# Storing the last three output tiles of an attention and feed-forward kernel from two queues in place of one

## The chip, the core and the metric

The kernel runs on one core of a Trainium2 chip. A core has four engines that compute: TensorE (PE, with its weight loads shown as PEld), VectorE (DVE), ScalarE (ACT) and GpSimd (POOL). SyncE (SP) computes nothing; in this kernel it issues nearly all transfers between the memory on the chip (SBUF) and the large memory outside it (HBM). [...] Each engine works through a list of its own in order. Engines wait for each other, and for transfers, by semaphores.

The metric is the device time of the core in microseconds (us), as the median of several executions. A profile is one further execution with the recorder on.

## What is computed

Attention over 576 positions with 16 extra "beacon" keys that every query may see, for 8 batches and 8 heads of width 64, followed by a gated feed-forward layer on the 4608 resulting rows:

```python
k_all = np.concatenate([beacon_k, k], axis=2)
v_all = np.concatenate([beacon_v, v], axis=2)
scores = scale * np.matmul(q, k_all.transpose(0, 1, 3, 2))
scores = np.where(causal, -1000000000.0, scores)
a = softmax(scores)
attn = np.matmul(a, v_all)                       # (8, 8, 576, 64)
x = attn.transpose(0, 2, 1, 3).reshape(4608, 512)
gate = np.maximum(x @ w_gate, 0.0)               # 512 -> 1536
val = x @ w_val
out = gate * val @ w_out                         # 4608 x 512, float32
```

## The kernel before

The attention's result is written, transposed, into one large tile `xT` (512 features in four groups of 128 partitions, 4608 columns). The feed-forward part takes the columns in pieces. For each batch it takes the first 512 of the 576 positions; the remaining 64 positions of the batches are gathered afterwards, four batches at a time, into two groups of 256 columns (the loop `for i in range(2)`, lines 899 to 908). The second of these groups (`i == 1`) is the last work of the kernel.

For a group of columns two functions are called:

- `hidden` (lines 822 to 843) computes the 1536 hidden features in 12 blocks of 128: four matmuls with `w_gate`, a Relu on ScalarE out of PSUM, four matmuls with `w_val`, and the product of both on VectorE, which goes to a tile `hT` in bfloat16.
- `project` (lines 845 to 867) multiplies the 12 `hT` tiles with `w_out` for 128 output rows: 12 matmuls into one PSUM bank (line 853), then one copy into an SBUF tile `osb` by ScalarE or VectorE (lines 861 and 862; the copy shows as line 438 on ScalarE and 440 on VectorE), then the stores to HBM (lines 864 to 867).

The 128 rows of a tile of the gathered groups belong to two batches, 64 rows each, which don't lie side by side in the output. Therefore such a tile has two stores of 64 rows (the list `rows` has two entries); a tile of the other kind has one store of 128 rows. The last tile of all is made in two halves of 256 columns (`LAST_PARTS = 2`), each with its own PSUM bank, copy and two stores. So the second gathered group ends with three output tiles: one of 128 x 512 and two of 128 x 256, and six stores.

Which engine does what, and in which order, is decided before the program is built. Each piece of work is a task with a set of engines that could do it, a cost, the tasks that it depends on, and a priority (class `Plan`, lines 146 to 264). The planner simulates the engines and repeatedly takes the task that could start earliest, the one of smallest priority value among equals. A copy may go to "ACT" or "DVE", whichever comes first in that simulation. Tasks of the engine "DMA" are issued by SP, with a simulated wire behind them. The order that the planner finds is the order of each engine's list. All six of the last stores are "DMA" tasks, so they stand in SP's list one after another.

An issue on SP ends when the transfer has been handed on; the transfer lands later and raises a semaphore. At the very end (the launch's line 941) SP waits for the landing of all transfers, one semaphore after another, and then the engines meet in a last barrier.

Of the kernel before, what the change touches and what calls it, by code (L numbers as in the profile page):

```python
# [51 lines left out]
OUT = -1300.0  # L52
# [93 lines left out]
class Plan:  # L146
# [7 lines left out]
    def add(self, engines, cost, run, deps=(), holds=(), prio=0.0, lag=None, part=False, lazy=0.0, after=0.0, move=0.0):  # L154
        t = Task(engines if isinstance(engines, tuple) else (engines,), cost, run, deps, holds, prio, lag, part, lazy, move)
        t.ready = after
        for d in t.deps:
            d.users.append(t)
        self.tasks.append(t)
        return t  # L160
# [107 lines left out]
def kernel(  # L268
# [12 lines left out]
    nc = tc.nc  # L281
    B, H, S, D = q.shape
# [4 lines left out]
    P = 128  # L287
# [65 lines left out]
    add = plan.add  # L353


    def c_dve(n):
        return 0.07 + 0.00104 * n
# [7 lines left out]
    def c_act(n):  # L365
        return 0.06 + 0.00083 * n
# [4 lines left out]
    def c_pe(n):  # L371
        return 0.003 + n / 2400.0
# [63 lines left out]
    def copy(e, dst, src):  # L436
        if e == "ACT":
            nc.scalar.copy(dst, src)  # L438
        elif e == "DVE":
            nc.vector.tensor_copy(dst, src)  # L440
        else:
            nc.gpsimd.tensor_scalar(dst, src, 1.0, 1.0, ALU.mult, ALU.mult)
# [379 lines left out]
    def hidden(rhs, w, c0, deps, hT, prio):  # L822
        hid = []
        for nf in range(NF):
            psg, psv, g = Hold(f_s, 2), Hold(f_s, 2), Hold(gate_s, 2)

            def product(w_r, ps, nf=nf):
                for ki in range(KM):
                    x = rhs(ki)
                    to = ps.tile[:, :w]  # L830
                    if len(x.shape) == 3:
                        to = to.rearrange("p (b s) -> p b s", b=x.shape[1])
                    nc.tensor.matmul(to, w_r[:, ki, nf * P:(nf + 1) * P], x, start=(ki == 0), stop=(ki == KM - 1))  # L833

            a = add("PE", 4 * c_pe(w), lambda _, f=product, ps=psg: f(wg_r, ps), deps + [weight_in["g", nf // 4]],
                    (psg,), prio + 0.02 * nf)
            r = add("ACT", c_act(w), lambda _, psg=psg, g=g: nc.scalar.activation(  # L837
                g.tile[:, :w], psg.tile[:, :w], AF.Relu), (a,), (psg, g), -1000 + prio)
            b_ = add("PE", 4 * c_pe(w), lambda _, f=product, ps=psv: f(wv_r, ps), [a, weight_in["v", nf // 4]],
                     (psv,), prio + 0.02 * nf + 0.01)  # L840
            hid.append(add("DVE", c_dve(w), lambda _, psv=psv, g=g, nf=nf: nc.vector.tensor_mul(  # L841
                hT[nf].tile[:, c0:c0 + w], g.tile[:, :w], psv.tile[:, :w]), (r, b_), (psv, g, hT[nf]), -1000 + prio))
        return hid

    def project(t0, rows, here, hT, prio, last):
        w = DM // LAST_PARTS if last else DM
        for n0 in range(0, DM, w):
            ps, osb = Hold(f_s, 4), Hold(osb_s, 1 + len(rows))
            prev = None
            for part in range(3):  # L850
                def outp(_, part=part, ps=ps, n0=n0):
                    for nf in range(4 * part, 4 * part + 4):
                        nc.tensor.matmul(ps.tile[:, :w], hT[nf].tile[:, t0:t0 + P], wo_r[:, nf, n0:n0 + w],  # L853
                                         start=(nf == 0), stop=(nf == NF - 1))

                need = [prev, weight_in["o", part]]
                for hid in here:
                    need += hid[4 * part:4 * part + 4] + (hid[:11] if part == 0 else [])
                prev = add("PE", 4 * c_pe(w), outp, need, (ps,) + tuple(hT[4 * part:4 * part + 4]),
                           prio + 0.3 + 0.01 * part + 0.001 * (n0 > 0) - (0.5 if part else 0))  # L860
            ev = add(("ACT", "DVE"), {"ACT": c_act(w), "DVE": c_dve(w)}, lambda x, ps=ps, osb=osb: copy(
                x.engine, osb.tile[:, :w], ps.tile[:, :w]), (prev,), (ps, osb), -1000 + prio)
            at = 0
            for r0, n in rows:
                add("DMA", (0.4, 0.78 * n / P), lambda _, osb=osb, r0=r0, n=n, at=at, n0=n0: nc.sync.dma_start(
                    out[r0:r0 + n, n0:n0 + w], osb.tile[at:at + n, :w]), (ev,), (osb,), prio + OUT)
                at += n


# [13 lines left out]
    def done(b, lo, hi):  # L883
        return [x for (b0, what, _), x in x_done.items() if b0 == b and SPAN[what][0] < hi and SPAN[what][1] > lo]

    REG = S // MT * MT
    for b in range(B):
        hT = [Hold(hid_s, len(CUTS.get(b, ())) + 1 + REG // P) for _ in range(NF)]
        cuts = [0, *CUTS.get(b, ()), REG]
        prio = 1000 + 10.0 * b  # L890
        here = []
        for a, z in zip(cuts, cuts[1:]):
            here.append(hidden(lambda ki, a=a, z=z, b=b: xT[:, ki, b * S + a:b * S + z], z - a, a, done(b, a, z), hT, prio))
            for t0 in range(a // P * P, z // P * P, P):
                project(t0, [(b * S + t0, P)], [x for x, c0, c1 in zip(here, cuts, cuts[1:]) if c0 < t0 + P and c1 > t0],
                        hT, prio, False)
            prio += 2.0
    ends = xT.rearrange("p k (b s) -> p k b s", s=S)
    for i in range(2):
        b0, b1 = i * B // 2, (i + 1) * B // 2  # L900
        w = (b1 - b0) * (S - REG)
        prio = 1000 + 10.0 * b1 - 5.0
        hT = [Hold(hid_s, 1 + w // P + (LAST_PARTS - 1) * i) for _ in range(NF)]
        deps = [x for b in range(b0, b1) for x in done(b, REG, S)]
        hid = hidden(lambda ki, b0=b0, b1=b1: ends[:, ki, b0:b1, REG:], w, 0, deps, hT, prio)
        for t0 in range(0, w, P):
            b = b0 + t0 // (S - REG)
            project(t0, [(x * S + REG, S - REG) for x in (b, b + 1)], [hid], hT, prio, i == 1 and t0 + P == w)

    def fill(n, to):  # L910
        for _ in range(n):
# [34 lines left out]
```

## Time and profile before

| | us |
|---|---|
| median of 3 runs | 409.17 |
| lowest and highest | 408.51, 409.42 |
| the profiled execution | 410.43 |
| its span, from the first to the last instruction | 408.7 |

The span is what the views of the profile divide up; all their times count from its start. The profiled execution took 1.73 us beyond its span. The page gives busy times by engine, a picture of the span in 40 slices of 10.2 us each, and the chain of work that ended last. A timeline row reads: start, duration, engine, line, operation, what it writes and reads, and in brackets how long the engine had been idle and who released it. SPq stands for SP's issues. The mean granted clock of TensorE was 0.997.

### The profile page before, as it was taken

The numbers are of one execution on the slowest core, as the hardware profiler recorded it, in microseconds if no ns is written. First come the engines' busy times: TensorE is split into PE (matmuls) and PEld (weight loads), VectorE is DVE, ScalarE is ACT, GpSimd is POOL, SyncE is SP. The second block draws the span as 40 slices with busy tenths as digits, with TensorE's granted clock in tenths as the row PEclk, the third lists the DMA queues.
The fourth block names the chain that finished last, engine by engine and source line by source line (L and its number), as shares of the span: only waits on it lengthen the run. The fifth ranks groups of instructions, "written<-read, shape, count | busy, mean of one in ns | idle before, by whom it ended". The sixth has DMA issues, their size and how long they took to land.

```text
span 408.7 us, 10376 instructions
## 1 busy us (share of the span) xinstructions
PE 394.1 (96%) x3276; PEld 246.8 (60%) x3311; DVE 315.8 (77%) x1159; ACT 289.9 (71%) x959; POOL 232.7 (57%) x434
## 2 busy tenths in 40 slices
PE   7899999989999999999999999999999999999994
PEld 5567867567766877555557754654554544444483
DVE  6898999889989988899998998787988544244251
ACT  6899989778888968797888799998867432033040
POOL 5899786947777667586975966875727200000000
PEclk9999999999999999999999999999999999999998
DMA  8899999999989999999999999999195730100112
GB/s 224 167 199 225 212 209 196 171 242 219 176 172 230 215 178 231 190 227 195 242 209 210 234 198 189 249 201 205 54 162 125 167 73 0 70 34 0 53 54 51
DMA packets 172616, 68.03 MB, mean 166 GB/s; under 512 B 146832, under 2 KB 168080, under 8 KB 172560
## 3 DMA queue, kind: packets, MB, share of 16 engines
q1 hardware_dynamic: 167808, 62.64, 75.5%
q0 software_dynamic: 4752, 4.72, 7.1%
q8 instruction: 26, 0.43, 0.5%
q14 instruction: 30, 0.25, 0.2%
HBM read 38.27 MB, written 9.44 MB: 117 GB/s over the span
## 4 chain that ended last, share of the span: by engine, by line
PE 84%; POOL 7%; DMA 2%; DVE 2%; ACT 2%; issue 2%; SPq 0%; POOLq 0%
PE f L833 42%; PE f L853 22%; PE f L663 7%; PE f L766 5%; PE f L497 4%; POOL xT L710 2%; POOL pb L710 2%; POOL h L486 2%; PE f L655 2%; DMA st<-in_beacon_k_dram 1%; PE f L795 1%; DMA st<-in_q_dram 1%; DVE diag L440 1%; PE f L745 1%; ACT xT L689 1%
## 5 line engine op out<-in xcount | busy, mean ns | idle before, releaser
L710 POOL TENSOR_SCALAR pb<-pb,small 128x576 bf16<-128x576 bf16 (+8 forms) x224 | 121.6, 557 | 56.0 <-DVE small L703 49.0
L689 ACT ACTIVATE pb<-f,small 128x64 bf16<-128x64 f32 (+6 forms) x256 | 131.0, 524 | 18.0 <-DVE small L678 13.1
L837 ACT ACTIVATE g<-f 128x512 f32<-128x512 f32 (+3 forms) x156 | 71.9, 470 | 67.9 <-PE f L833 66.6
L678 DVE CUSTOM_DVE_ANT_0 f<-f,mask 128x128 f32<-128x128 f32 (+7 forms) x256 | 112.0, 477 | 9.4 <-PE f L663 7.2
L833 PE MATMUL f<-xT,wv_r 128*128 128x512 bf16 (+3 forms) x616 | 111.8, 313 | 0.5
L833 PE MATMUL f<-xT,wg_r 128*128 128x512 bf16 (+3 forms) x619 | 109.5, 313 | 0.3
L841 DVE TENSOR_TENSOR hT<-g,f 128x512 bf16<-128x512 f32 (+3 forms) x156 | 80.5, 520 | 37.6 <-PE f L833 34.4
L853 PE MATMUL f<-wo_r,hT 128*128 128x512 bf16 (+1 forms) x423 | 102.0, 373 | 1.0
L833 PEld LDWEIGHTS <-wg_r 128*128 128x128 bf16 x624 | 60.0, 98 | 32.3 <-issue 0.2
L833 PEld LDWEIGHTS <-wv_r 128*128 128x128 bf16 x624 | 59.4, 98 | 33.0 <-issue 0.8
L853 PEld LDWEIGHTS <-hT 128*128 128x128 bf16 x444 | 41.6, 98 | 39.1
L689 ACT ACTIVATION_READ_ACCUMULATOR pb<-f,small 128x1 f32 x256 | 53.8, 210 | 0.0
L663 PE MATMUL f<-kT,diag 128*128 128x384 bf16 (+7 forms) x255 | 46.9, 286 | 1.9 <-DVE diag L440 0.8
L678 DVE DVE_READ_ACCUMULATOR2_ANT small<- 128x1 f32 x296 | 41.6, 141 | 0.2 <-issue 0.2
L486 POOL TENSOR_SCALAR h<-st 128x512 bf16<-128x512 f32 x62 | 37.8, 614 | 7.1 <-DMA st<-in_q_dram 2.9
L440 DVE COPY osb<-f 128x512 f32<-128x512 f32 (+1 forms) x26 | 17.6, 678 | 23.2 <-PE f L853 22.7
L710 POOL TENSOR_SCALAR xT<-xT,small 128x64 bf16<-128x64 bf16 (+4 forms) x64 | 26.9, 436 | 7.7 <-ACT xT L689 4.1
L497 PE MATMUL f<-ident,h 128*128 128x128 bf16 (+2 forms) x320 | 28.1, 217 | 2.8 <-POOL h L486 2.5
L438 ACT CAST diag<-f 64x512 bf16<-64x512 f32 (+2 forms) x52 | 23.0, 442 | 9.6 <-PE f L497 4.1
L497 PEld LDWEIGHTS <-h 128*128 128x128 bf16 (+2 forms) x320 | 20.3, 98 | 15.6 <-POOL h L486 7.9
L440 DVE CAST diag<-f 64x512 bf16<-64x512 f32 (+2 forms) x44 | 26.3, 598 | 4.2 <-ACT diag L438 2.0
L663 PEld LDWEIGHTS <-diag 128*128 128x128 bf16 x256 | 20.4, 98 | 15.0 <-issue 1.5
(67 smaller groups left out, 376.7 us busy)
## 6 DMA issues: line engine op xcount, KB each, us to landing
st<-in_q_dram SPq DMA_DIRECT2D x32, 256.0 KB, 4.5
st<-in_k_dram SPq DMA_DIRECT2D x32, 256.0 KB, 5.0
out_dram<-osb SPq DMA_DIRECT2D x32, 256.0 KB, 2.6
st<-in_v_dram SPq DMA_DIRECT2D x24, 256.0 KB, 4.7
st<-in_v_dram SPq DMA_DIRECT2D x8, 224.0 KB, 4.9
wg_r<-in_moe_w_gate_dram POOLq DMA_DIRECT2D x3, 512.0 KB, 8.5
wv_r<-in_moe_w_val_dram POOLq DMA_DIRECT2D x3, 512.0 KB, 10.3
wo_r<-in_moe_w_out_dram POOLq DMA_DIRECT2D x3, 512.0 KB, 14.2
```

Source lines behind the costliest of these rows:

```text
L438: nc.scalar.copy(dst, src)
L440: nc.vector.tensor_copy(dst, src)
L486: (nc.gpsimd if x.engine == "POOL" else nc.vector).tensor_scalar(to, of, by, 1.0, ALU.mult, ALU.mult)
L497: nc.tensor.matmul(to, h16.tile[:rows, a * P:(a + 1) * P], ident[:rows, :rows], start=True, stop=True)
L663: nc.tensor.matmul(view(i), t.diag.tile[:, p, j * P:j * P + P], kT[:, p, :n], start=True, stop=True)
L678: nc.vector.tensor_tensor_reduce(out=view(i), in0=view(i), in1=msk, scale=1.0, scalar=small["t"][:, 0:1] if name in "EF" else 3.0e38, op0= ...
L689: nc.scalar.activation(ph.tile.rearrange("p a n -> p (a n)")[:, a:a + n], view(i), AF.Exp, bias=small["t"][:, low:low + 1], scale=-1.0, ac ...
L710: (nc.gpsimd if x.engine == "POOL" else nc.vector).tensor_scalar(one, one, small["t"][:, 8 + i:9 + i], 1.0, ALU.mult, ALU.mult)
L833: nc.tensor.matmul(to, w_r[:, ki, nf * P:(nf + 1) * P], x, start=(ki == 0), stop=(ki == KM - 1))
L837: r = add("ACT", c_act(w), lambda _, psg=psg, g=g: nc.scalar.activation(g.tile[:, :w], psg.tile[:, :w], AF.Relu), (a,), (psg, g), -1000 + ...
L841: hid.append(add("DVE", c_dve(w), lambda _, psv=psv, g=g, nf=nf: nc.vector.tensor_mul(hT[nf].tile[:, c0:c0 + w], g.tile[:, :w], psv.tile[: ...
L853: nc.tensor.matmul(ps.tile[:, :w], hT[nf].tile[:, t0:t0 + P], wo_r[:, nf, n0:n0 + w], start=(nf == 0), stop=(nf == NF - 1))
```

## The change

`project` gets one more argument, `final`, which is true for the second gathered group alone. There, the store of the second 64 rows of a tile (`at` is 64 then) becomes a task of the engine "ACT" with a cost of 0.6, and the function that runs it issues the transfer on ScalarE's queue. All other stores stay as they were. The second gathered group has three tiles, so three stores move.

```diff
-    def project(t0, rows, here, hT, prio, last):
+    def project(t0, rows, here, hT, prio, last, final):
...
             for r0, n in rows:
-                add("DMA", (0.4, 0.78 * n / P), lambda _, osb=osb, r0=r0, n=n, at=at, n0=n0: nc.sync.dma_start(
-                    out[r0:r0 + n, n0:n0 + w], osb.tile[at:at + n, :w]), (ev,), (osb,), prio + OUT)
+                def store(x, osb=osb, r0=r0, n=n, at=at, n0=n0):
+                    (nc.scalar if x.engine == "ACT" else nc.sync).dma_start(out[r0:r0 + n, n0:n0 + w], osb.tile[at:at + n, :w])
+
+                if final and at:
+                    add("ACT", 0.6, store, (ev,), (osb,), prio + OUT)
+                else:
+                    add("DMA", (0.4, 0.78 * n / P), store, (ev,), (osb,), prio + OUT)
                 at += n
...
-                        hT, prio, False)
+                        hT, prio, False, False)
...
-            project(t0, [(x * S + REG, S - REG) for x in (b, b + 1)], [hid], hT, prio, i == 1 and t0 + P == w)
+            project(t0, [(x * S + REG, S - REG) for x in (b, b + 1)], [hid], hT, prio, i == 1 and t0 + P == w, i == 1)
```

## The prediction

> **What bounds the kernel now.** I read the page first: the span, the busy shares, the slices, the chain.
>
> ```profile
> span 408.7 us, 10376 instructions
> PE 394.1 (96%) x3276; PEld 246.8 (60%) x3311; DVE 315.8 (77%) x1159; ACT 289.9 (71%) x959; POOL 232.7 (57%) x434
> ...
> PE   7899999989999999999999999999999999999994
> ...
> DMA  8899999999989999999999999999195730100112
> ...
> PE 84%; POOL 7%; DMA 2%; DVE 2%; ACT 2%; issue 2%; SPq 0%; POOLq 0%
> ```
>
> TensorE is busy for 96% of the span and makes 84% of the chain. But its last slice of 10.2 us shows 4 tenths, and there the DMA engines wake up again. The change acts only in that slice, so I went on to the chain and the timeline of the end.
>
> ```profile
> 403.23 0.02 issue
> 403.26 0.42 DVE osb L440
> ```
>
> ```profile
> 401.51 0.69 DVE L440 COPY osb<-f 128x512 f32<-128x512 f32 x1 [2.97 <-PE f L853]
> 401.95 0.37 ACT L438 COPY osb<-f 128x256 f32<-128x256 f32 x1 [3.95 <-PE f L853]
> 403.26 0.42 DVE L440 COPY osb<-f 128x256 f32<-128x256 f32 x1 [1.05 <-PE f L853]
> ```
>
> The chain of waits ends at 403.68 (403.26 + 0.42), with the last copy out of PSUM, yet the span ends at 408.7. So 5.0 us lie behind the last computing instruction, where the chain follows nothing. There SyncE (SP) works off the stores. Its rows, one by one (start, duration of the issue):
>
> ```profile
> 402.23 0.51 SPq L865 DMA_DIRECT2D out_dram<-osb  x1
> 402.79 0.58 SPq L865 DMA_DIRECT2D out_dram<-osb  x1
> 403.46 0.55 SPq L865 DMA_DIRECT2D out_dram<-osb  x1
> 404.07 0.59 SPq L865 DMA_DIRECT2D out_dram<-osb  x1
> 404.75 0.55 SPq L865 DMA_DIRECT2D out_dram<-osb  x1
> 405.35 0.59 SPq L865 DMA_DIRECT2D out_dram<-osb  x1
> ```
>
> These are the stores of the last three tiles, two halves each; I call the tiles X (128x512), Y and Z (128x256) and the halves 1 (first 64 rows) and 2. X is ready at 402.20 (401.51 + 0.69) and Y at 402.32, but Y1 is issued at 403.46 only. Z is ready at 403.68 and Z1 goes out at 404.75, Z2 at 405.35: SP is behind by 1.1 and 1.7 us. The queue of issues, not the copies, sets the end. What follows the last issue:
>
> ```profile
> SPq L941 <- DMA out_dram<-osb: 1.4, 1, 1.4
> ```
>
> ```profile
> 403.38:404.78 1.40, 0.00 (x0) 0.00 (x0) 0.30 (x1) 0.00 (x0) 0.00 (x0) 1.00 0.92 200
> 405.30:405.78 0.48, 0.00 (x0) 0.00 (x0) 0.00 (x0) 0.00 (x0) 0.00 (x0) 1.00 0.64 137
> 405.94:406.42 0.48, 0.00 (x0) 0.00 (x0) 0.00 (x0) 0.00 (x0) 0.00 (x0) 0.84 0.64 137
> 406.58:407.05 0.47, 0.00 (x0) 0.00 (x0) 0.00 (x0) 0.00 (x0) 0.00 (x0) 0.50 0.65 140
> 383.50:384.40 0.90, 0.90 (x6) 0.42 (x5) 0.01 (x1) 0.00 (x0) 0.00 (x0) 1.00 0.81 298
> ```
>
> The last two numbers of a window are the DMA engines' share and GB/s. Z2's issue ends at 405.94, its 64 KB move from 406.58 to 407.05 (0.64 later, for 0.47), and SP, which waits from 405.98 or so, is released 1.4 later, at 407.40 (0.35 after the last packet). From there to the end of the span is 1.3 us of closing checks and barriers at line 941.
>
> **The change part by part.** In the order of the changed program, PE, VectorE and GpSimd have the same instructions in the same order; SP has three stores fewer; ScalarE gets X2, Y2 and Z2 behind its copy of Y, its last work. So nothing before 402 us moves, and nothing is queued behind the new stores on ScalarE but the closing barrier.
>
> *SP loses three issues.* X1 stays at 402.23 to 402.74. Y1 follows after the gap of 0.09 that stands between 403.37 and 403.46 (a second wait): 402.83, until 403.42 at the most. Then SP waits for Z's copy, and Z1 starts 0.03 after it, as X1 did after X's: 403.71. That is 1.64 us ahead of 405.35, where the last issue starts now.
>
> *ScalarE gains three issues.* No transfer of this program is issued on ScalarE, so the price is bounded by the nearest rows: 0.33 us (SP, a store of 128 rows) and 0.93 (GpSimd, loads of weights).
>
> ```profile
> L865 SPq DMA_DIRECT2D out_dram<-osb x4: 332/332/333, 382.7 to 388.7; - x4
> ```
>
> ```profile
> 16.09 0.93 POOL L455 DMA_DIRECT2D wg_r<-in_moe_w_gate_dram  x1
> ```
>
> I take SP's 0.51 to 0.59 for a store of 64 rows, the same shape on a like queue. X2 then starts between 402.23 and 402.35 (when the copy of Y ends), Y2 ends by 403.6, before Z is ready, and Z2 starts beside Z1 at 403.71. At 0.93 Z2 starts at 402.23 + 2 x (0.93 + 0.09) = 404.27 and lands at 404.27 + 0.93 + 0.64 + 0.47 + 0.35 = 406.66, still 0.74 before the present end.
>
> *The closing checks.* They take the landings one after another:
>
> ```profile
> L941 SPq EVENT_SEMAPHORE  x8: 28/28/28, 407.4 to 407.8; - x8
> ```
>
> Eight checks lie between 407.4 and 407.8. Z1 on SP keeps the place that is checked first, Z2 on ScalarE takes the last, so Z2 may land 0.4 later at no cost. The checks still run, 1.3 us in all.
>
> *The data.* Halves 1 and 2 of a tile now move at the same time. Z1 and Z2 end their issues at 404.22 to 404.30, and their packets start 0.64 later, at about 404.9. Whether they run side by side or one behind the other isn't in the trace, which has one queue. Below: side by side, 0.47, a landing at 404.86 + 0.47 + 0.35 = 405.68, a gain of 1.72. Above: all six stores packed behind one another at a full share of the engines, from 403.38: 1.40 x 0.92 + 4 x 0.48 x 0.64 = 2.52, to 405.90, a landing at 406.25, a gain of 1.15. A row speaks for the better half: a store of 128 rows (both halves) ran at 298 GB/s with a share of 0.81, the 64-row halves of X at 200 GB/s with 0.92, so halves of opposite partitions seem to get in each other's way less than rows of the same one. I take the middle, 1.45.
>
> [...]
>
> **Sum.** Against the profiled execution: 410.43 us, of which 408.7 is span and 1.73 lies around it; it becomes 408.98, its span 407.25. That execution is 1.26 above the median of 409.17, and I take the same difference there: 409.17 - 1.45 = 407.72.
>
> **The rivals.**
>
> *A, one descriptor generator for both queues.* The issues end at 402.74, 403.37, 404.01, 404.66, 405.30 and 405.94: 0.64 apart each time, though the gaps before them are 0.05 to 0.10. Longer gap, shorter issue (0.55 after 0.09, 0.59 after 0.06). Something behind SP keeps a pace of 0.64, and the first store, with nothing ahead of it, took only 0.51. If that something serves ScalarE too, with h per store, the sixth issue ends at 402.74 + 5h against 405.94: at h = 0.64 nothing is gained (409.17), at 0.585 0.27, at 0.51 0.65 (408.5). My value is 0.54, 0.50 gained, 408.7. Against it: loads of four times as much data show no such pace, three of them in 1.46, 0.49 each.
>
> ```profile
> 2.83 1.46 SPq L520 DMA_DIRECT2D st<-in_k_dram  x3
> ```
>
> So the 0.64 may as well be SP's own work on an odd shape. [...]
>
> *B, the data serialize.* If the DMA engines never overlap two of the six stores, they take 1.40 + 4 x 0.48 = 3.32 from 403.38, to 406.70, a landing at 407.05: 0.35 gained, 408.8. Against it: with a share of 0.64 in each burst there is room, and now already Y1's packets start while X2's end, since 1.40 reaches to 404.78 and Y1's issue ended at 404.01, 0.64 before 404.65.
>
> *C, slower: ScalarE's issues are long.* If one takes a, Z2 starts at 402.23 + 2(a + 0.09), and lands at 403.87 + 3a. It decides from 407.8 (with the 0.4 of the last check), at a = 1.31, and costs 3 us for each further us; from a = 1.58 the loss is over 0.2%. What speaks for it: this queue is used nowhere else in the program, and an issue of SP did take 2.47 once, early, behind a long row of loads:
>
> ```profile
> 9.51 2.47 SPq L562 DMA_DIRECT2D st<-in_k_dram  x1
> ```
>
> At 2.47 the loss is 3.48, 412.6. Against it: at the end no other transfer is under way, and all SP's stores take 0.33 to 0.59.
>
> **How the numbers follow.** My forecast 0.52; A 0.24; B 0.10; C 0.14. The predicted time is the forecast's, 407.7. Its own range is 1.15 to 1.72 gained, 407.45 to 408.0, and with the spread of the three runs (408.51 to 409.42, 0.45 to a side) 407.1 to 408.4. The range given goes on to A and B, whose slowest is 409.17, and the spread: 407.1 to 409.6; C is left out. 0.2% is 0.82 us, about what a measurement of this kernel can tell from no change: faster than 408.35 is 0.95 of the forecast, and a little of A (h below 0.48) and of B, 0.55 in all; within 0.2% the rest of these, 0.31; slower is C, 0.14.
>
> **What would show it.** In the profile after: SP's last store starts at 403.7 and not 405.3, and the first wait of line 941 ends near 406.0 and not 407.4; three issues on ScalarE of 0.5 to 0.6 each, Z2 at 403.7. Where A holds, issues that overlap in time are longer, 0.8 to 1.3, on both queues, and their ends stand 0.5 to 0.64 apart counted over both. Where B holds, the issues are short but Z's landings come 2.5 us or more after them. Where C holds, ScalarE's rows are over 1.3. The prediction is wrong if anything before 402 us moves, or if the closing part after the last landing grows beyond 1.3 us by a second queue.

## The result and the profile after

| | before | changed |
|---|---|---|
| median of 14 runs each, us | 409.43 | 407.38 |
| lowest and highest | 408.51, 411.38 | 406.69, 409.22 |
| the profiled execution | 410.43 | 408.14 |
| its span | 408.7 | 406.4 |

The ratio of the changed kernel to the one before is 0.9954, with a 95% interval of 0.9938 to 0.9971: 1.9 us faster, 1.2 to 2.5 by the interval. The same two kernels were timed again later on one chip (the last experiment below) and gave 0.9970, 0.9958 to 0.9982, 1.2 us. The prediction was 407.7, 1.45 us faster.

The page of the changed kernel has a new transfer queue with the three moved stores, 0.26 MB of them:

```profile
span 406.4 us, 10379 instructions
...
q1 hardware_dynamic: 167568, 62.38, 75.2%
...
q10 hardware_dynamic: 240, 0.26, 0.2%
```

The timeline of its end, first the copies (`osb<-f`, out of the PSUM tile that the matmuls of line 853 write), then the issues one by one (start, duration):

```profile
400.76 0.69 DVE L440 COPY osb<-f 128x512 f32<-128x512 f32 x1 [2.97 <-PE f L853]
401.19 0.37 ACT L438 COPY osb<-f 128x256 f32<-128x256 f32 x1 [3.95 <-PE f L853]
402.50 0.42 DVE L440 COPY osb<-f 128x256 f32<-128x256 f32 x1 [1.05 <-PE f L853]
```

```profile
401.48 0.51 SPq L866 DMA_DIRECT2D out_dram<-osb  x1
402.08 0.54 SPq L866 DMA_DIRECT2D out_dram<-osb  x1
402.96 0.47 SPq L866 DMA_DIRECT2D out_dram<-osb  x1
...
401.48 0.55 ACTq L866 DMA_DIRECT2D out_dram<-osb  x1
402.13 0.78 ACTq L866 DMA_DIRECT2D out_dram<-osb  x1
403.00 0.56 ACTq L866 DMA_DIRECT2D out_dram<-osb  x1
```

Z's copy ends at 402.93. Both queues are free by then (SP since 402.62, ScalarE since 402.91), and Z1 and Z2 go out 0.03 and 0.07 us after it. Before, Z1 and Z2 went out 1.07 and 1.67 us after it. What follows the issues, as SP's waits, the data's windows (last two numbers: share of the DMA engines, GB/s) and the closing checks of line 946:

```profile
SPq L946 <- DMA out_dram<-osb: 1.5, 1, 1.5
```

```profile
402.63:403.71 1.08, 0.00 (x0) 0.00 (x0) 0.30 (x1) 0.00 (x0) 0.00 (x0) 1.00 0.96 255
403.72:404.82 1.10, 0.00 (x0) 0.00 (x0) 0.00 (x0) 0.00 (x0) 0.00 (x0) 1.00 0.80 224
404.20:404.82 0.62, 0.00 (x0) 0.00 (x0) 0.00 (x0) 0.00 (x0) 0.00 (x0) 1.00 0.83 210
```

```profile
L946 SPq EVENT_SEMAPHORE  x8: 27/28/28, 405.0 to 405.5; - x8
```

The first window holds most of X, at 255 GB/s where it was 200; by the stamps of their packets X's two halves move from 402.64 to 403.81, in 1.17 us in place of 1.40. Y and Z follow up to 404.81, where they took four bursts up to 407.05. The third window lies in Z's stretch: 210 GB/s, against 137 and 140 for the bursts of its two halves before. SP is released by Z1's landing at 405.02, 2.09 after Z's copy, and the eight checks and the barrier follow as before, 1.3 us.

The two profiles differ by 2.3 us of span, but not all of that is the change. Z's copy ends at 402.93 here and at 403.68 before, though no instruction up to there differs; over all runs of this study it ended anywhere from 401.5 to 403.7. What belongs to the change is the time from Z's copy to the end. The trace's unrounded stamps give it for every kernel of the study that moves whole 64-row stores (the changed kernel, profiled once more, gave 0.07, 2.26 and 3.41):

| us after the end of Z's copy | last issue starts | last landing | end of the span |
|---|---|---|---|
| before: six on SP | 1.67 | 3.71 | 5.04 |
| changed: three and three | 0.07 | 2.25 | 3.42 |
| all six on ScalarE | 1.72 | 3.81 | 5.15 |
| Z2 alone on ScalarE | 1.06 | 3.08 | 4.41 |
| X2 and Y2 on ScalarE | 0.55 | 2.59 | 3.92 |
| second halves on GpSimd | 0.30 | 2.64 | 3.97 |
| second halves not stored | 0.03 | 1.96 | 2.99 |
| changed, last checks in another order | 0.07 | 2.24 | 3.22 |

The change is worth 5.04 - 3.42 = 1.62 us by this table. That lies within both intervals of the timed runs.

### The profile page after: what moved, and what is told of

Same layout as the page of the kernel before. It is cut to its first block, busy times and chain, and to the rows that moved or that the text cites. A ratio compares the mean times of both kernels' runs of the same rounds, so it can differ in the third digit from the quotient of the medians.

```text
span 406.4 us, 10379 instructions
## 1 busy us (share of the span) xinstructions
PE 393.1 (97%) x3276; PEld 246.4 (61%) x3311; DVE 315.0 (78%) x1159; ACT 290.3 (71%) x959; POOL 233.3 (57%) x434
## 4 chain that ended last, share of the span: by engine, by line
PE 83%; POOL 7%; DMA 5%; ACT 1%; issue 1%; DVE 1%; SPq 0%; POOLq 0%; DVEq 0%
PE f L833 42%; PE f L853 22%; PE f L663 7%; PE f L766 5%; DMA st<-in_v_dram 4%; PE f L497 3%; POOL xT L710 3%; PE f L655 2%; POOL pb L710 1%; DMA st<-in_beacon_k_dram 1%; PE f L795 1%; POOL h L486 1%; PE f L658 1%; ACT xT L689 1%; POOL v L442 1%
## 6 DMA issues: line engine op xcount, KB each, us to landing
wv_r<-in_moe_w_val_dram POOLq DMA_DIRECT2D x3, 512.0 KB, 10.1
```

## The experiments

**All six on ScalarE.** One queue again, but the other one.

```diff
-                if final and at:
+                if final:
                     add("ACT", 0.6, store, (ev,), (osb,), prio + OUT)
```

> All six stores of the last three tiles on ScalarE's queue, SP has none. Measure: from the end of the last copy (tile Z) to the last landing; it is 3.71 us in the kernel before and 2.25 in the changed one. Theory (one queue of issues is the limit, two queues work side by side): with all six on one queue the gain is gone, the last issue starts about 1.7 us after Z's copy and the last landing is 3.7 after it, time equal to the kernel before within 0.3 us; if the 0.78 us of one ScalarE issue is that queue's own price, up to 4.6. Rival (ScalarE's queue is simply quicker to land, or the gain came from SP being relieved before the end): last landing 2.1 to 2.5 after Z's copy, as in the changed kernel.

The time was 409.80 against 409.24 of before, ratio 1.0010 (0.9989 to 1.0031). ScalarE's issues in its profile (duration as smallest, median, largest in ns), and the time from issue to landing:

```profile
L866 ACTq DMA_DIRECT2D out_dram<-osb x6: 552/580/617, 400.8 to 404.0; - x6
...
DMA to landing us min/median/max: 2.0/2.1/2.4
```

The gain is gone: the last landing is 3.81 us after Z's copy. Neither ScalarE's queue nor an empty SP brings anything by itself; two queues do. ScalarE alone keeps the same pace from issue to issue as SP alone, 0.63 us ((403.985 - 400.813) / 5 by the unrounded stamps), so the pace is no peculiarity of SP. The run also prices ScalarE's issue of 64 rows at 0.55 to 0.62 us, some 0.03 above SP's, so the 0.78 of Y2 in the changed kernel is not that queue's own price.

**Only Z2 on ScalarE.**

```diff
-                if final and at:
+                if final and at and last and n0:
```

> Only the very last store (Z2) goes to ScalarE, SP keeps five. Theory: SP is still behind, Z1 starts about 1.07 us after Z's copy and lands 3.1 after it; one pace of 0.64 us of the gain remains out of 1.6. Rival (a shared generator with a backlog serves both queues in turn): Z2, though issued at once, waits behind SP's backlog, its issue takes over 0.8 us, and the last landing stays near 3.7.

The ratio was 0.9972 (0.9948 to 0.9995). The timeline of its end:

```profile
400.06 3.06 SPq L866 DMA_DIRECT2D out_dram<-osb  x5
401.08 0.42 DVE L440 COPY osb<-f 128x256 f32<-128x256 f32 x1 [1.06 <-PE f L853]
401.54 0.56 ACTq L866 DMA_DIRECT2D out_dram<-osb  x1
```

Z2 starts 0.03 us after the copy (401.08 + 0.42 = 401.50), amid SP's row of five, and its issue takes 0.56, no longer than with ScalarE alone. SP's last issue ends at 403.12, 1.6 after the copy, and sets the end. The gain is 5.04 - 4.41 = 0.63, one issue's pace, as the theory had it. A backlog that served both queues in turn would have held Z2 up.

**X2 and Y2 on ScalarE, both halves of Z on SP.**

```diff
-                if final and at:
+                if final and at and not n0:
```

> X2 and Y2 go to ScalarE, both halves of Z to SP. Theory: SP is free when Z is ready, Z1 starts 0.03 us and Z2 0.67 us after Z's copy, last landing 2.7 after it, a gain of 1.0 us. Rival (the data of two queues get in each other's way): the last landing is no earlier than 3.0 because Z no longer overlaps and Z2's landing still takes over 2.3 from its issue.

The ratio was 0.9976 (0.9957 to 0.9996). Z2 starts 0.55 after the copy, lands at 2.59, and the gain is 1.12; expected were 0.67, 2.7 and 1.0. Z2's landing takes 2.05 from its issue, as before, so what the other queue moved earlier doesn't hold up the end. X2 and Y2 do land later beside SP's stores, 2.72 and 2.63 us after their issues where SP alone took 2.36 and 2.04 (0.19 of Y2's is its longer issue): the data of two queues get in each other's way, but not in what ends last here. The second issue of ScalarE is long here too:

```profile
401.24 0.77 ACTq L866 DMA_DIRECT2D out_dram<-osb  x1
```

**The second halves not stored.** Half of the last three tiles is left out, so this kernel's time stands for SP's three stores alone. From here on a diff shows the added lines alone. In this run and the next five all stores are tasks of the engine "DMA" in the plan, whichever queue issues them.

```diff
+                    if not (final and at):
+                        nc.sync.dma_start(out[r0:r0 + n, n0:n0 + w], osb.tile[at:at + n, :w])
```

> The second 64 rows of the last three tiles are not stored at all; SP's three stores are alone. Theory: Z1 starts 0.03 us after Z's copy and lands 2.0 after it, against 2.09 in the changed kernel, so ScalarE's stores cost SP's at most 0.1 us. Rival (the data of the two halves serialize): Z1 lands 0.3 us or more earlier than in the changed kernel, 1.8 or less. On ScalarE's slow issue of 0.78 us it says nothing.

Z1's row in its profile, a single issue:

```profile
L867 SPq DMA_DIRECT2D out_dram<-osb x1: 466/466/466, 403.5 to 403.5; - x1
...
DMA to landing us min/median/max: 1.9/1.9/1.9
```

Alone, Z1 lands 1.96 us after the copy; beside ScalarE's stores it lands 2.09 after it. The second half of the data costs the first 0.13 us (Z2 itself lands 0.16 after Z1), between the 0.1 and the 0.3 that the two theories expected, and nearer to the first.

**24 stores of 16 rows, on one queue and on two.** A long row shows the pace of a queue, and whether two share it. `ON_BOTH` stands here for the constant of the run: False with SP alone, True with both.

```diff
+                    for s in range(0, n, 16 if final else n):
+                        m = 16 if final else n
+                        (nc.scalar if final and at and ON_BOTH else nc.sync).dma_start(
+                            out[r0 + s:r0 + s + m, n0:n0 + w], osb.tile[at + s:at + s + m, :w])
```

> The last three tiles are stored in pieces of 16 rows, 24 stores in all, every one on SP: a long row of issues that shows the pace of one queue. Theory: 0.55 to 0.65 us from issue to issue, whatever the bytes (16 KB or 32 KB and not 64 or 128), so the last issue ends about 24 x 0.6 - 1.45 = 13 us after Z's copy. Rival (the pace is set by the bytes or the rows, not by the issue): about a quarter of 0.64 each, the end near that of the kernel before.

> The same 24 stores, 12 on SP (first halves) and 12 on ScalarE (second halves). Theory (two independent queues): each keeps its own 0.55 to 0.65, issues last as long as with SP alone, the last ends 12 x 0.62 - 1.45 = 6 us after Z's copy. Rival (one generator serves both, and only a short row of stores hides it): over both queues together one issue each 0.5 to 0.64 us, each issue 1.0 to 1.2 long, the end near 13 us as with SP alone. In between, if a part of an issue is shared: the 0.78 us issue of Y2 in the changed kernel would be the rule from the second pair on, some 0.4 us per issue over both, the end near 8 us.

The timeline of the one with SP alone, then of the one with both:

```profile
401.81 10.98 SPq L868 DMA_DIRECT2D out_dram<-osb  x24
```

```profile
401.80 5.44 SPq L868 DMA_DIRECT2D out_dram<-osb  x12
...
401.81 5.58 ACTq L868 DMA_DIRECT2D out_dram<-osb  x12
```

On SP alone 24 issues take 10.98 us, 0.46 from one to the next. That misses the expected 0.55 to 0.65: a store of 16 rows is cheaper to issue than one of 64. With two queues 24 issues take 5.58, and SP's half keeps its 0.46. For this shape neither queue holds up the other.

**16 stores of 64 rows by 128 columns, on one queue and on two.** The same for the shape of the case, with a quarter to a half of the bytes.

```diff
+                    c = 128 if final else w
+                    for s in range(0, w, c):
+                        (nc.scalar if final and at and ON_BOTH else nc.sync).dma_start(
+                            out[r0:r0 + n, n0 + s:n0 + s + c], osb.tile[at:at + n, s:s + c])
```

> The last three tiles in pieces of 64 rows by 128 columns, 16 stores, all on SP. Theory: the pace of 0.64 us belongs to the 64 rows (four rows for each DMA engine), not to the bytes, so it stays 0.6 to 0.65 with a half to a quarter of the bytes, and the last issue ends about 16 x 0.64 - 1.45 = 8.8 us after Z's copy. Rival (the bytes set it): 0.46 or less, as with the 16-row pieces, end below 6.

> The same 16 stores, 8 on SP and 8 on ScalarE. It tells what the 0.78 us of ScalarE's Y2 issue in the changed kernel is. If both queues share something that a store of 64 rows needs longer than one of 16: issues of 0.7 to 0.8 come back on ScalarE's queue and the common pace is 0.35 to 0.45 us an issue, the end at 5 to 6 us after Z's copy. If it was the bytes of X (2 KB rows that were still under way): no issue above 0.65, each queue keeps its 0.64, the end near 8 x 0.64 - 1.45 = 3.7 us.

The timeline of the one with SP alone; of the one with both, the two rows as a whole, the issues' durations, and ScalarE's second issue:

```profile
402.09 10.10 SPq L868 DMA_DIRECT2D out_dram<-osb  x16
```

```profile
400.95 5.00 SPq L868 DMA_DIRECT2D out_dram<-osb  x8
...
400.95 5.33 ACTq L868 DMA_DIRECT2D out_dram<-osb  x8
...
L868 SPq DMA_DIRECT2D out_dram<-osb x8: 509/586/606, 400.9 to 405.4; - x8
L868 ACTq DMA_DIRECT2D out_dram<-osb x8: 552/608/828, 401.0 to 405.7; - x8
...
401.55 0.83 ACTq L868 DMA_DIRECT2D out_dram<-osb  x1
```

With SP alone the pace is (10.10 - 0.6) / 15 = 0.63, as with four times the bytes: it belongs to the 64 rows. With both, 16 issues take 5.33 us, and SP keeps its pace, (5.00 - 0.6) / 7 = 0.63. Neither branch of the expectation holds as it was put. A long issue comes back, 0.83, so the bytes of X are not its cause; but it comes once, on ScalarE's second issue, and all later ones are at 0.62 or less. ScalarE's second issue ends at 402.38 and its row at 406.28, 0.33 us after SP's; the six issues after the long one take (406.28 - 402.38) / 6 = 0.65 us each, about the pace of one queue alone. What lengthens the second issue, no run shows; the first pair, which starts within 0.01 us, isn't lengthened, nor the pair of Z1 and Z2 in the changed kernel, which starts within 0.05.

**The second halves on GpSimd's queue.**

```diff
+                    (nc.gpsimd if final and at else nc.sync).dma_start(out[r0:r0 + n, n0:n0 + w], osb.tile[at:at + n, :w])
```

> X2, Y2 and Z2 on GpSimd's queue in place of ScalarE's. Theory (any second queue that is free relieves SP): SP's rows as in the changed kernel, Z1 lands 2.1 us after Z's copy; GpSimd's issues last 0.8 to 0.95, Z2 starts 0.3 to 0.5 after Z's copy, lands 2.8 to 3.2 after it, a gain of 0.8 to 1.2 us in place of 1.6. Rival (GpSimd's transfers start or land later than the two other queues'): Z2 lands 3.7 or more after Z's copy, no gain.

The ratio was 0.9959 (0.9937 to 0.9980). The issues in its profile, and the time to landing over all six:

```profile
L866 SPq DMA_DIRECT2D out_dram<-osb x3: 466/507/542, 400.2 to 401.6; - x3
L866 POOL DMA_DIRECT2D out_dram<-osb x3: 527/570/597, 400.4 to 401.9; - x3
...
DMA to landing us min/median/max: 2.3/2.6/3.2
```

GpSimd's issues are cheaper than expected (0.53 to 0.60, not 0.8 to 0.95), but start 0.3 us after the data are ready, and SP's own stores land later beside them: Z1 takes 2.46 us, where it took 2.06 beside ScalarE's. The gain is 5.04 - 3.97 = 1.07 by the profile, as expected; the timed runs can't tell it from the changed kernel's 1.62.

**Another order of the last checks.** In the run without the second halves, the end came 1.03 us after the last landing; in the kernel before it was 1.33, and in the changed one 1.33 after Z1's. The difference is where that landing stands among the eight checks: first where it is 1.33, sixth where it is 1.03. In the long rows of issues above, with the last landing in second place, it is 1.28, and in third 1.22. The semaphores go round in the order of the stores: in the trace of the kernel before, the six stores raise 104 to 108 and then 101, and the checks take 101 first and 108 last. GpSimd's loads raise others there, 111 to 118, so moving one earlier store to GpSimd moves Z1 from the first place to the last.

```diff
+                    moved = r0 == (B - 1) * S + 3 * P
+                    (nc.scalar if x.engine == "ACT" else nc.gpsimd if moved else nc.sync).dma_start(
+                        out[r0:r0 + n, n0:n0 + w], osb.tile[at:at + n, :w])
```

> The changed kernel, and the store of the last tile of 128 rows before the end (issued some 14 us before the last copy) goes to GpSimd, which is idle by then. That store then takes a semaphore of GpSimd's transfers, and the six last stores move up one place in the order in which the closing checks take their landings: Z1 is checked last and Z2 last but one, where now Z1 is checked first. Theory (after Z1's landing the closing checks themselves are on the path, 8 of them 0.06 us apart, 0.5 us to the drain): last landing as in the changed kernel, 2.25 us after Z's copy, but the end of the span 0.2 us sooner, 3.2 after Z's copy in place of 3.42; too little for the medians to tell from the changed kernel. Rival (the closing part is a fixed 1.33 us after the last landing that SP waits for, or GpSimd's transfer holds up the end): 3.4 or more.

> The changed kernel once more beside the one above, on the same chip: from Z's copy to the end of the span 3.4 us, to the last landing 2.25, ScalarE's second issue 0.78 again; Z's copy itself ends anywhere from 401.5 to 403.7, as it did in the runs so far whose instructions up to there are the same.

SP's waits in its profile, now three short ones in place of one of 1.5:

```profile
SPq L948 <- DMA out_dram<-osb: 1.3, 3, 0.5
```

The end of the span comes 3.22 us after Z's copy, the last landing 2.24; the changed kernel beside it has 3.41 and 2.26. The medians are 407.06, 407.35 and 408.69 for this one, the changed one and the one before (ratios 0.9963, 0.9950 to 0.9977, and 0.9970, 0.9958 to 0.9982). So it beats the kernel before; its 0.2 us over the changed kernel are seen in the trace alone.

## Why the prediction was right

**The bound.** The tail behind the last copy was set by SP's queue of issues. The run with all six on ScalarE shows it: the work is the same, one queue is full again, and the gain is gone. The run with Z2 alone moved gives back one pace, 0.63, of it.

**SP's three issues.** Z1 was to start 0.03 after Z's copy; it did (402.96). The 1.64 us from there stand.

**ScalarE's three issues.** The price of 0.51 to 0.59, taken over from SP, held for X2 and Z2 (0.55, 0.56). Y2 took 0.78. It ended at 402.91, just before Z was ready, so the error cost nothing but 0.04 us at Z2's start; a last copy 0.2 us earlier would have met a busy queue.

**The closing checks.** Z2 landed 0.16 us after Z1, within the 0.4 that it could be late. The end came 1.33 us after the landing that is checked first, as before, so the second queue didn't lengthen the closing part. That Z1 stands first in the checks and pays for all eight of them was in the working as a fact, and could have been read as a saving: it is worth 0.2 us.

**The data.** This is the term that was mis-sized. Between 1.15 and 1.72 I took 1.45, which puts 0.27 us on the meeting of the halves. Counted to the last landing of all, Z2's, that came out: 3.71 - 2.25 = 1.46, a loss of 0.26, of which 0.09 is Z2's issue, which ends later than I had assumed. But Z2 is checked last, so its 0.16 behind Z1 cost nothing; the working had this slack, and the sum didn't use it. What counts is Z1's landing, 3.71 - 2.09 = 1.62, so 0.1 for the meeting of the halves. By their packets Z1's data moved from 404.10 to 404.59 and Z2's from 404.39 to 404.81, 0.71 us for both, where one alone took 0.46 before: neither side by side (0.47) nor one behind the other (0.94), but half and half. That the middle of the two bounds was right for Z2 is luck, since no row gave it. The row that I named, 298 GB/s for a store of both halves against 200 for the halves of one, was no closer: X moved at 255 GB/s, between the two.

**The sum.** 407.72 was forecast from the first median of 409.17, and 407.38 measured against 409.43. The 1.62 of the trace accounts for 1.2 to 2.5 as measured; the rest of the difference is no effect that these runs show. Z's copy did end 0.75 us earlier in the changed profile, and I had named a move before 402 us as a sign of being wrong; as the engines' lists up to the copy are the same and kernels with the same lists ended it 2.2 us apart, a single pair of profiles can't give that sign.

**Rival A** fell, all but a piece. Had both queues shared the pace of one, 16 issues of 64 rows would have taken 10.1 us, as they did on SP alone; on two queues they took 5.33. The even 0.64 from issue to issue, on which the rival rested, belongs to one queue and to 64 rows, on ScalarE as on SP. The piece is ScalarE's second issue, 0.2 us longer than alone (0.77 to 0.83, against 0.55 to 0.62 with all six on ScalarE); no run shows why.

**Rival B** fell as it was priced: Z1 lands 2.06 us after its issue, and not 2.5; X and the rest move at 255 and 224 GB/s. A part of it is there: X2 is issued with X1, but its packets start 0.63 us after X1's, and Z's two halves share 0.2 of their 0.71 us. In this trace the halves serialize in part, which costs Z1 0.13 us (it lands 2.09 after Z's copy, 1.96 without the second halves). What the second queue saved is time to issue: the last issue starts 0.07 us after Z's copy in place of 1.67, which is the 1.6 us.

**Rival C** fell: no issue on ScalarE took over 0.83. What the working set against it, that all SP's stores take 0.33 to 0.59, is so only for the end: three stores between 80 and 180 us took 0.91 to 1.08, and 2.47 was not SP's longest issue either (a load at 47.82 us took 6.56).

## What to carry to other kernels

Where a chain ends several microseconds before the span does (5.04 us here), list the transfers' issues behind it one by one: here a row of issues on one queue started up to 1.67 us later than their data were ready, a bound that no engine's busy time showed. Spread them so that every queue is free when the last data arrive, which gave 1.62 us; moving only the last one, or only the earlier ones, gave 0.63 and 1.12 of it. To size so small a change, measure from the last common instruction to the end in the profile, since the time before it wandered by 2.2 us between runs of the same instructions.

## What the hardware showed unexpectedly

The price of an issue on SP followed the shape, not the bytes, and not simply the number of rows: 0.33 us for 128 rows of 2 KB (eight stores after 350 us; earlier ones up to 1.08), 0.47 to 0.61 for 64 rows of 512 bytes, 1 KB or 2 KB in the last stores, 0.34 to 0.42 for 16 rows. Where SP and ScalarE issued 64-row stores at the same moment, ScalarE's second issue took 0.77 to 0.83 us, 0.2 more than alone, and the two then ran side by side (5.33 us for 16 issues, 10.1 on SP alone). Beside GpSimd's stores landings were slower: Z1's came 2.46 us after its issue, 2.06 beside ScalarE's, and the slowest of the six took 3.2, against 2.72. Data of two queues overlapped in part: 0.71 us for the two halves of Z, 0.46 for one. And the closing checks took 0.06 us each (eight from 405.04 to 405.47), so the transfer that landed last was best checked last: 3.22 us from Z's copy to the end in place of 3.42, in the trace alone.
